# Top-32 attention: folding the scores twice before the search for the 32nd largest

## The chip, the cores and the metric

One core of a Trainium2 chip. The metric is the device time of one execution in microseconds, as the median of the runs shown.

## What is computed

Eight batches of eight heads, 576 tokens, head dimension 64. In every row of scores all but the 32 largest are masked, the rest goes through softmax and meets V. A feed-forward with a squared ReLU follows. Cut to what matters:

```python
scores = scale * np.matmul(q, k.transpose(0, 1, 3, 2))
kth = np.partition(scores, -32, axis=-1)[..., -32:-31]
scores = np.where(scores >= kth, scores, -1000000000.0)
attn = softmax(scores) @ v                  # (8, 8, 576, 64)
x = attn.transpose(0, 2, 1, 3).reshape(4608, 512)
out = np.maximum(x @ w_in, 0.0) ** 2 @ w_out    # 512 -> 2048 -> 512
```

So for each of 8 x 8 x 576 rows the 32nd largest of 576 numbers is needed, exactly.

## The kernel before

The kernel is written as a plan. `build` (L363) records every operation with its engine, an assumed duration, a priority (a due time), the tiles it reads, writes and takes, and the operations it must follow. `Plan.schedule` (L117) plays the plan through once, on the host, with the assumed durations, and thereby lays down the order of instructions on each engine; each engine's list is then emitted in that order, with semaphore waits where an operation needs another engine's or its own earlier result (`Emitter`, L204). On the chip nothing is reordered any more: an engine that waits holds up all that stands behind it.

Work is cut into pairs of heads (32 of them, `load_pair`, L371) and row blocks of 128 query rows, nine a pair, 288 in all. A pair's blocks are handled in four groups (`top_k`, L424): three with two blocks, the last with three (the third holds the 64 remaining rows of both heads). For a group:

- TensorE (PE) computes the scores into PSUM, ScalarE (ACT) copies them to `s` (L456), 128 x 576 in fp32.
- VectorE (DVE) takes `m`, the maximum of the left and the right half of `s` (L479), 288 columns. GpSimd (POOL) gets the minima as exact integers on the bit patterns: the sum of the halves `t1` (L476), and `lo` = `t1` - `m` (L482).
- On `m` DVE runs four rounds of MAX8 (L489, the eight largest of each row, sorted) with three MATCH_REPLACE8 between them (L494, these eight overwritten by -3e38): 32 largest of the maxima, in `a`. Each MATCH_REPLACE8 comes with a short MATCH_VALUE_LOAD. One MAX8 on `lo` (L500) gives the eight largest minima, `b8all`.
- A tiny minimum and a tiny reduction (L508, L511) merge the two sorted lists into `kth`, the 32nd largest of all 576, for the whole group.
- ACT makes the mask `w` from `s` and `kth` (L519).

`attend` (L538) adds the mask on PE in the transposed scores, ACT takes exp, PE multiplies with V; ACT copies the result (`av`), DVE takes a reciprocal of the row sums (`rzall`, L622), POOL multiplies (`x`, L624), PE transposes. `feed` (L644) is the feed-forward of a batch, spread over the next batch's top-k work; its squares run on ACT, in the last two batches on POOL (L678), at the very end on DVE. POOL also casts V (`vb`, L417, L420) and, in the first batch, the weights (L770).

`verdict` (L774) raises a flag if any row's result could be wrong (the eighth minimum is over the 32nd found); then a second, full program of the same tiling is run, which makes no such assumption. `PER` (L354) is the time per block by which priorities are spaced.

Of the kernel before, what the change touches and what calls it, by code (L numbers as in the profile page):

```python
# [12 lines left out]
P = 128  # L13
# [71 lines left out]
class Plan:  # L85
# [3 lines left out]
    def op(self, eng, dur, prio, fn, r=(), w=(), u=(), take=(), after=(), order=(), sem=None, ndma=0, nbf=0.0):  # L89
# [13 lines left out]
        for t in list(r) + list(w) + list(u):  # L103
            t.ops.append(o)
            t.left += 1
# [4 lines left out]
        o.later = ({t.taker for t in list(r) + list(w) + list(u)} | set(order)) - deps - {o, None}  # L110
        o.deps = deps
        o.wars = [t for t in list(w) + list(u)]
        o.tiles = list(r) + list(w) + list(u)
# [163 lines left out]
def bass_top_k_attn__then__act_relu_squared_kernel(  # L277
# [10 lines left out]
    HALF = S // 2  # L288
# [9 lines left out]
    def sb(name, shape, dt=FP32, n=None):  # L298
# [8 lines left out]
    b8all = sb("b8all", [P, NALL, 8])  # L307
    kth = sb("kth", [P, NALL])
# [45 lines left out]
    PER = 3.65  # L354
# [8 lines left out]
    def build(full, weights, pl):  # L363
        state = {"n": 0, "u": 0}
# [59 lines left out]
        def top_k(gi, qk, tg, dw):  # L424
# [36 lines left out]
            bt = tile("b") if full else None  # L461
            m, wk, t1, lo = ([tile(nm) for _ in range(nb)] for nm in ("m", "wk", "t1", "lo"))
            dk = [0]

            def dve(dur, fn, **kw):
                dk[0] += 1
                return pl.op("dve", dur, tg + .37 * dk[0], fn, **kw)

            def A(i, r):
                return at(a)[:, i, 8 * r:8 * r + 8]  # L470

            def B(i, r):
# [12 lines left out]
            last = [None] * nb  # L485
            for rnd in range(4):
                src = m if rnd == 0 else wk
                for i in range(nb):
                    last[i] = dve(.365, lambda i=i, rnd=rnd, src=src: vec.max(A(i, rnd), at(src[i])[:, :]),  # L489
                                  r=[src[i]], w=[a])  # L490
                if rnd == 3:
                    break
                for i in range(nb):
                    f = lambda i=i, rnd=rnd, src=src: vec.match_replace(  # L494
                        at(wk[i])[:, :], A(i, rnd), at(src[i])[:, :], NEG)
                    if rnd == 0:
                        dve(.425, f, r=[m[i]], w=[wk[i]], take=[wk[i]], after=[last[i]])
                    else:
                        dve(.425, f, u=[wk[i]], after=[last[i]])
            bl = [dve(.365, lambda i=i: vec.max(B(i, 0), at(lo[i])[:, :]), r=[lo[i]], w=[bt] if full else [])  # L500
                  for i in range(nb)]
            if full:
                bl = [dve(.425, lambda i=i: vec.match_replace(at(lo[i])[:, :], B(i, 0), at(lo[i])[:, :], NEG),
                          u=[lo[i]], after=[bl[i]]) for i in range(nb)]
                bl = [dve(.365, lambda i=i: vec.max(B(i, 1), at(lo[i])[:, :]), r=[lo[i]], w=[bt], after=[bl[i]])
                      for i in range(nb)]
            nr = 16 if full else 8
            mn = dve(.1, lambda: vec.tensor_tensor(  # L508
                at(a)[:, 0:nb, 32:32 + nr], at(bt)[:, 0:nb, 0:16] if full else b8all[:, n0:n0 + nb, :],
                at(a)[:, 0:nb, 30:30 - nr:-1], ALU.min), u=[a], r=[bt] if full else [], after=bl)  # L510
            kt = dve(.1, lambda: vec.tensor_reduce(  # L511
                kth[:, n0:n0 + nb], at(a)[:, 0:nb, 31:32 + nr], AX.X, ALU.max, negate=full), r=[a], after=[mn])
            kths.append(kt)
# [357 lines left out]
```

## Time and profile before

| | |
|---|---|
| median of 3 runs | 1114.63 us (1114.40 to 1114.79) |
| the profiled execution, its own time | 1116.01 us |
| its span (first to last instruction) | 1114.2 us |
| DVE busy | 1054.0 us (95%) |
| PE busy | 936.5 us (84%) |
| ACT busy | 772.7 us (69%) |
| POOL busy | 614.4 us (55%) |
| mean granted TensorE clock | 0.945 of full speed |

Busy times are unions of an engine's instructions; an instruction that has been issued and is held up inside its engine counts as busy. The profile's line of an operation is the line of the kernel before; a lambda's line is the line of the instruction in it.

### The profile page before, as it was taken

Reading aid. Unit: us, or ns where it says so; the run is one execution under the profiler, and the core shown is the slowest. Engines: PE = TensorE matmul, PEld = TensorE weight load, DVE = VectorE, ACT = ScalarE, POOL = GpSimd, SP = SyncE. Lnnn points to the kernel's source line nnn. Section 1 sums busy time; section 2 is a strip of 40 time slices with the busy share of each in tenths; the row PEclk is TensorE's granted clock in tenths of the full one; section 3 lists DMA queues with packets and bytes.
Section 4 is the critical chain, followed back from the end, with each engine's and each line's share of the span. In section 5 each row is a group of like instructions: output and inputs, shape, how many; then the busy total and the mean of one; then the engine's idle time right before and its main releaser. Section 6 shows DMA issues by size and latency. Waiting matters only on the chain.

```text
span 1114.2 us, 23090 instructions
## 1 busy us (share of the span) xinstructions
PE 936.5 (84%) x8082; PEld 551.0 (49%) x8082; DVE 1054.0 (95%) x3791; ACT 772.7 (69%) x1341; POOL 614.4 (55%) x815
## 2 busy tenths in 40 slices
PE   5767667989888997979878998888978899679997
PEld 3444434545455454645545554554445455445554
DVE  5999999999999999999999999999999999999961
ACT  4555657866788667976778676796678866567562
POOL 6775554555645555455545555545555455676461
PEclk8788888999989999999989999999998999989999
DMA  6851110111301121010301022011111000000001
GB/s 165 229 165 33 34 26 7 33 31 35 76 3 31 41 69 33 12 32 30 90 12 33 29 54 59 2 34 51 52 39 33 2 29 16 1 1 11 30 16 37
DMA packets 124414, 47.73 MB, mean 43 GB/s; under 512 B 116608, under 2 KB 116608, under 8 KB 124288
## 3 DMA queue, kind: packets, MB, share of 16 engines
q1 hardware_dynamic: 124288, 46.16, 16.2%
q8 instruction: 65, 1.06, 0.4%
q14 instruction: 61, 0.50, 0.2%
HBM read 36.70 MB, written 9.44 MB: 41 GB/s over the span
## 4 chain that ended last, share of the span: by engine, by line
DVE 79%; PE 14%; ACT 4%; issue 1%; DMA 1%; POOL 1%; SPq 0%; POOLq 0%
DVE a L489 31%; DVE wk L494 27%; PE ps L358 13%; DVE m L479 10%; DVE b8all L500 8%; ACT w L519 2%; DVE a L508 1%; DVE kth L511 1%; ACT s L456 1%; DVE rzall L622 1%; DMA rq<-in_q_dram 1%; POOL lo L482 0%; ACT av L620 0%; SPq L377 0%; DMA rk<-in_k_dram 0%
## 5 line engine op out<-in xcount | busy, mean ns | idle before, releaser
L358 PE MATMUL ps<-qk 64*128 64x288 f32 (+7 forms) x2640 | 442.9, 448 | 81.7 <-ACT s L456 42.2
L482 POOL TENSOR_TENSOR lo<-t,m 128x288 int32<-128x288 int32 x288 | 251.1, 887 | 330.9 <-DVE a L508 240.0
L489 DVE MAX8 a<-wk 128x8 f32<-128x288 f32 x864 | 344.9, 442 | 0.0
L358 PEld LDWEIGHTS ps<-qk 64*128 64x128 f32 (+1 forms) x2640 | 219.6, 187 | 204.6 <-ACT s L456 59.8
L519 ACT ACTIVATE w<-s,kth 128x576 bf16<-128x576 f32 x288 | 214.4, 771 | 123.4 <-DVE kth L511 122.9
L494 DVE MATCH_REPLACE8 wk<-a,wk 128x288 f32<-128x288 f32 x576 | 249.1, 438 | 0.0
L476 POOL TENSOR_TENSOR t<-s 128x288 int32<-128x288 int32 x288 | 227.9, 807 | 22.3 <-ACT s L456 19.9
L581 ACT ACTIVATE p<-ps 128x640 bf16<-128x640 f32 (+1 forms) x192 | 154.7, 809 | 77.2 <-PE ps L358 76.5
L456 ACT COPY s<-ps 128x576 f32<-128x576 f32 x288 | 171.0, 641 | 37.5 <-PE ps L358 36.2
L358 PE MATMUL ps<-xt,win 128*128 128x288 bf16 (+2 forms) x1088 | 151.9, 290 | 25.3 <-ACT g L665 14.0
L479 DVE TENSOR_TENSOR m<-s 128x288 f32<-128x288 f32 x288 | 152.8, 531 | 13.4 <-ACT s L456 13.4
L358 PE MATMUL ps<-wo,g 128*128 128x512 bf16 (+1 forms) x640 | 161.9, 381 | 2.5 <-ACT s L456 2.2
L358 PEld LDWEIGHTS ps<-steep_bf,w 128*128 128x128 bf16 (+1 forms) x1600 | 83.6, 102 | 112.6 <-issue 111.7
L358 PEld LDWEIGHTS ps<-xt,win 128*128 128x128 bf16 x1088 | 97.4, 101 | 65.4 <-ACT g L665 17.4
L494 DVE MATCH_REPLACE8 wk<-a,m 128x288 f32<-128x288 f32 x288 | 124.6, 438 | 0.0
L358 PE MATMUL ps<-steep_bf,w 128*128 128x128 bf16 (+3 forms) x1600 | 124.1, 222 | 0.0
L489 DVE MAX8 a<-m 128x8 f32<-128x288 f32 x288 | 115.8, 442 | 0.2
L500 DVE MAX8 b8all<-lo 128x8 f32<-128x288 f32 x288 | 114.8, 439 | 0.0
L624 POOL TENSOR_TENSOR x<-av,rzall 128x256 bf16<-128x256 f32 (+2 forms) x68 | 44.9, 660 | 78.5 <-DVE rzall L622 72.9
L358 PEld LDWEIGHTS ps<-wo,g 128*128 128x128 bf16 (+1 forms) x640 | 54.3, 100 | 60.2 <-issue 11.8
L665 ACT ACTIVATE g<-ps 128x576 bf16<-128x576 f32 x112 | 72.5, 649 | 13.6 <-PE ps L358 12.8
L358 PE MATMUL ps<-vb,p 128*128 128x65 bf16 (+1 forms) x1600 | 62.8, 195 | 6.1 <-ACT p L594 6.0
(52 smaller groups left out, 641.1 us busy)
## 6 DMA issues: line engine op xcount, KB each, us to landing
rq<-in_q_dram SPq DMA_DIRECT2D x64, 128.0 KB, 2.4
rk<-in_k_dram SPq DMA_DIRECT2D x64, 128.0 KB, 2.5
rv<-in_v_dram SPq DMA_DIRECT2D x64, 128.0 KB, 2.4
out_dram<-o SPq DMA_DIRECT2D x32, 256.0 KB, 2.0
ws<-in_moe_w_in_dram SPq DMA_DIRECT2D x8, 512.0 KB, 4.4
ws<-in_moe_w_out_dram SPq DMA_DIRECT2D x8, 512.0 KB, 4.4
rq<-in_q_dram SPq DMA_DIRECT2D x32, 32.0 KB, 2.4
rk<-in_k_dram SPq DMA_DIRECT2D x32, 32.0 KB, 2.5
```

The source lines that it names most:

```text
L358: return pe.matmul(o, l, r, start=start, stop=stop, skip_group_check=True)
L456: pl.op("act", .64, tg - 28 + i, lambda i=i: act.copy(at(st[i])[:, :].rearrange("p (a c) -> p a c", a=2), ps32[:, ss[i].slot:ss[i].slot + ...
L476: pl.op("gp", .81, tg - 1 + .8 * i, lambda i=i: gp.tensor_tensor(at(t1[i])[:, :].bitcast(I32), at(st[i])[:, 0:HALF].bitcast(I32), at(st[i] ...
L479: dve(.42, lambda i=i: vec.tensor_tensor(at(m[i])[:, :], at(st[i])[:, 0:HALF], at(st[i])[:, HALF:S], ALU.max), r=[st[i]], w=[m[i]], take=[ ...
L482: pl.op("gp", .88, tg + .8 + .8 * i, lambda i=i: gp.tensor_tensor(at(lo[i])[:, :].bitcast(I32), at(t1[i])[:, :].bitcast(I32), at(m[i])[:, ...
L489: last[i] = dve(.365, lambda i=i, rnd=rnd, src=src: vec.max(A(i, rnd), at(src[i])[:, :]), r=[src[i]], w=[a])
L494: f = lambda i=i, rnd=rnd, src=src: vec.match_replace(at(wk[i])[:, :], A(i, rnd), at(src[i])[:, :], NEG)
L500: bl = [dve(.365, lambda i=i: vec.max(B(i, 0), at(lo[i])[:, :]), r=[lo[i]], w=[bt] if full else []) for i in range(nb)]
L519: pl.op("act", .75, tw + .8 * i, lambda i=i: act.activation(at(ws[i])[:, :], at(st[i])[:, :], ACTF.Relu, bias=kth[:, n0 + i:n0 + i + 1], s ...
L581: return act.activation(o, i, ACTF.Exp, scale=0.125)
L624: pl.op("gp", .15 + .16 * nu, tt + 4, lambda: gp.tensor_tensor(at(xr)[:, 0:nu, :], at(avs)[:, 0:nu, 0:64], rzall[:, u0:u0 + nu].unsqueeze( ...
L665: return act.activation(at(g)[:, 0:nt].rearrange("p (a c) -> p a c", a=2), ps32[:, hh.slot:hh.slot + 2, 0:hw], ACTF.Relu)
```

## The change

Scores are folded twice. DVE takes `m` as before and then `pp`, the maximum of the two halves of `m` (144 columns: the largest of each four scores). POOL builds both kinds of minima by integer sum and subtraction: `t2` = sum of the halves of `m`, the middle ones `t2` - `pp`, and the low ones `t1` - `m`. All three go into one tile `f` of 576 columns: what is left of `pp` in columns 0 to 143, the middle ones in 144 to 287, the low ones in 288 to 575.

The rounds: MAX8 and MATCH_REPLACE8 on `pp` (144 columns), again on `f[0:144]`, again on `f[0:288]` (after the middle minima are there), and a fourth MAX8 on all 576 (after the low ones), whose eighth is the 32nd largest. MAX8 writes its eight in reverse order into `kth`, so that the eighth stands in the block's column and the next block of its kind overwrites the other seven. L508 and L511 go. The flag is raised where `kth` is over the 16th or the 24th found. Each block's mask now waits for its own last MAX8. The pools of tiles change (`f` of 576 columns x 4, `pp` x 4, `m` 4 instead of 3, `t2` x 2; `wk`, `lo`, `b` go), `PER` is 3.2 instead of 3.65, and since durations and dependences changed the schedule lays all engines' orders down anew. The second program, which runs only when the flag is raised, gets four rounds on 576 columns. The core of the diff:

```diff
-        "s": ([P, S], FP32, 8), "m": ([P, HALF], FP32, 3), "wk": ([P, HALF], FP32, 3),
-        "t1": ([P, HALF], FP32, 2), "lo": ([P, HALF], FP32, 3), "a": ([P, 3, 48], FP32, 3),
-        "b": ([P, 3, 16], FP32, 2), "sh": ([P, 3], FP32, 2), "w": ([P, S], BF16, 13),
+        "s": ([P, S], FP32, 8), "m": ([P, HALF], FP32, 4), "pp": ([P, QUART], FP32, 4),
+        "t1": ([P, HALF], FP32, 2), "t2": ([P, QUART], FP32, 2), "f": ([P, S], FP32, 4),
+        "a": ([P, 3, 8], FP32, 3), "sh": ([P, 3], FP32, 2), "w": ([P, S], BF16, 13),
...
-    PER = 3.65
+    PER = 3.2
...
+            def eighth(t, i):
+
+                return t[:, i, ix[i] + 7:(ix[i] - 1 if ix[i] else None):-1]
...
-            for i in range(nb):
-                pl.op("gp", .81, tg - 1 + .8 * i, lambda i=i: gp.tensor_tensor(
-                    at(t1[i])[:, :].bitcast(I32), at(st[i])[:, 0:HALF].bitcast(I32),
-                    at(st[i])[:, HALF:S].bitcast(I32), ALU.add), r=[st[i]], w=[t1[i]], take=[t1[i]])
...
-                pl.op("gp", .88, tg + .8 + .8 * i, lambda i=i: gp.tensor_tensor(
-                    at(lo[i])[:, :].bitcast(I32), at(t1[i])[:, :].bitcast(I32),
-                    at(m[i])[:, :].bitcast(I32), ALU.subtract), r=[t1[i], m[i]], w=[lo[i]], take=[lo[i]])
-            for rnd in range(4):
...
+                def whole(dur, prio, i, op, o, x, y, **kw):
+                    return pl.op("gp", dur, prio + .8 * i, lambda: gp.tensor_tensor(
+                        o().bitcast(I32), x().bitcast(I32), y().bitcast(I32), op), **kw)
...
+                    whole(.81, tg - 1, i, ALU.add, L, A, B, r=[st[i]], w=[t1[i]], take=[t1[i]])
+                    dve(.42, lambda i=i, A=A, B=B: vec.tensor_tensor(at(m[i])[:, :], A(), B(), ALU.max),
+                        r=[st[i]], w=[m[i]], take=[m[i]])
...
+                    whole(.46, tg - .5, i, ALU.add, L, M1, M2, r=[m[i]], w=[t2[i]], take=[t2[i]])
+                    dve(.27, lambda i=i, M1=M1, M2=M2: vec.tensor_tensor(at(pp[i])[:, :], M1(), M2(), ALU.max),
+                        r=[m[i]], w=[pp[i]], take=[pp[i], f[i]] + ([a] if i == 0 else []))
+                for i in range(nb):
+                    mid.append(whole(.48, tg + .5, i, ALU.subtract, lambda i=i: at(f[i])[:, QUART:HALF],
+                                     lambda i=i: at(t2[i])[:, :], lambda i=i: at(pp[i])[:, :],
+                                     r=[t2[i], pp[i]], w=[f[i]]))
+                    low.append(whole(.88, tg + 2.5, i, ALU.subtract, lambda i=i: at(f[i])[:, HALF:S],
+                                     lambda i=i: at(t1[i])[:, :], lambda i=i: at(m[i])[:, :],
+                                     r=[t1[i], m[i]], w=[f[i]]))
...
+                    prev[i] = [dve(.215, lambda i=i: vec.max(at(a)[:, i, :], at(pp[i])[:, :]), r=[pp[i]], w=[a])]
...
+                    prev[i] = [dve(.275, lambda i=i: vec.match_replace(
+                        at(f[i])[:, 0:QUART], at(a)[:, i, :], at(pp[i])[:, :], NEG),
+                        r=[pp[i]], hold=[a], w=[f[i]], after=prev[i])]
+                for t, wd, dur, more in ((c16, QUART, .215, None), (c24, HALF, .365, mid)):
+                    for i in range(nb):
+                        prev[i] = [chain(t, i, prev[i] + ([more[i]] if more else []), dur,
+                                         lambda i=i, t=t, wd=wd: vec.max(eighth(t, i), at(f[i])[:, 0:wd]),
+                                         hold=[f[i]])]
+                    for i in range(nb):
+                        prev[i] = [chain(t, i, prev[i], dur + .06, lambda i=i, t=t, wd=wd: vec.match_replace(
+                            at(f[i])[:, 0:wd], eighth(t, i), at(f[i])[:, 0:wd], NEG), hold=[f[i]])]
+                for i in range(nb):
+                    ks.append(chain(kth, i, prev[i] + [low[i]], .665, lambda i=i: vec.max(
+                        eighth(kth, i), at(f[i])[:, :]), hold=[f[i]]))
```

What the schedule makes of it. A group of two blocks on DVE in the middle of the kernel before (`a` holds the eights, `wk` the worked-down maxima):

```order
L479 TENSOR_TENSOR m<-s 128x288
L508 TENSOR_TENSOR a<-b8all,a 128x2x8
L479 TENSOR_TENSOR m<-s 128x288
L511 TENSOR_REDUCE kth<-a 128x2
L489 MAX a<-m 128x8 x2
L494 MATCH_REPLACE wk<-a,m 128x288 x2
L489 MAX a<-wk 128x8 x2
L494 MATCH_REPLACE wk<-a,wk 128x288
L622 RECIPROCAL rzall<-av 128x5
```

L508 and L511 there belong to the group before. The same place after the change, a whole group (`c` stands for both c16 and c24, the eights of rounds two and three):

```order
L522 TENSOR_TENSOR m<-s 128x288 x2
L528 TENSOR_TENSOR pp<-m 128x144 x2
L539 MAX a<-pp 128x8 x2
L541 MATCH_REPLACE f<-a,pp 128x144 x2
L547 MAX c<-f 128x8 x2
L550 MATCH_REPLACE f<-c,f 128x144 x2
L547 MAX c<-f 128x8 x2
L550 MATCH_REPLACE f<-c,f 128x288 x2
L553 MAX kth<-f 128x8 x2
```

The four two-input instructions m, m, pp, pp now stand one behind the other at the head of a group; nothing is left of the merge at its end. POOL in the middle of the kernel before:

```order
L482 TENSOR_TENSOR lo<-t,m 128x288 x2
L476 TENSOR_TENSOR t<-s 128x288 x2
L417 CAST vb<-rv 128x8x64
L624 TENSOR_TENSOR x<-av,rzall 128x320
L420 TENSOR_SCALAR vb<-rv,heads 128x64 x2
```

And after (`t<-s` is the sum of the halves of s, `t<-m` that of the halves of m, `f<-t,pp` the middle and `f<-t,m` the low minima), from the low minima of a group of two through the head of the group of three behind it:

```order
L514 TENSOR_TENSOR f<-t,m 128x288
L663 TENSOR_TENSOR x<-av,rzall 128x320
L514 TENSOR_TENSOR f<-t,m 128x288
L514 TENSOR_TENSOR t<-s 128x288 x2
L419 CAST vb<-rv 128x8x64
L514 TENSOR_TENSOR t<-m 128x144 x2
L514 TENSOR_TENSOR f<-t,pp 128x144
L514 TENSOR_TENSOR t<-m 128x144
L514 TENSOR_TENSOR f<-t,pp 128x144 x2
```

Between a group's sums (done before its m) and its low minima, POOL now has the two instructions on 144 columns for each block. In the last batch the squares of the feed-forward (`g<-g`) stand among these, on POOL:

```order
L717 TENSOR_TENSOR g<-g 128x576
L514 TENSOR_TENSOR f<-t,m 128x288 x2
L663 TENSOR_TENSOR x<-av,rzall 128x320
L717 TENSOR_TENSOR g<-g 128x576 x3
L514 TENSOR_TENSOR t<-s 128x288
L514 TENSOR_TENSOR t<-m 128x144
L514 TENSOR_TENSOR t<-s 128x288
```

In the kernel before they stand in the same way between `lo` and `t1`, one or two at a time.

## Rows read from the trace of the kernel before

**Rows 1.** The page: busy us (share of the span) and instructions of each engine.
```profile
PE 936.5 (84%) x8082; PEld 551.0 (49%) x8082; DVE 1054.0 (95%) x3791; ACT 772.7 (69%) x1341; POOL 614.4 (55%) x815
```

**Rows 2.** Stretches of the span: length, busy us (x instructions) of PE, PEld, DVE, ACT, POOL; clock, DMA.
```profile
150.00:950.00 800.00, 699.32 (x6040) 407.36 (x6040) 793.92 (x2874) 596.57 (x1027) 424.83 (x558) 0.96 0.14 35
...
1000.00:1114.00 114.00, 103.83 (x996) 61.55 (x994) 77.20 (x272) 65.09 (x127) 54.06 (x71) 0.99 0.07 23
```

**Rows 3.** Timeline of DVE, 500 to 507 us: start, length, instruction.
```profile
501.05 0.07 DVE L494 MATCH_VALUE_LOAD wk<-a,wk 128x8 f32 x1
...
501.48 1.17 DVE L489 MAX8 a<-wk 128x8 f32<-128x288 f32 x3
502.56 0.07 DVE L494 MATCH_VALUE_LOAD wk<-a,wk 128x8 f32 x1
...
506.07 0.43 DVE L479 TENSOR_TENSOR m<-s 128x288 f32<-128x288 f32 x1
506.43 0.17 DVE L508 TENSOR_TENSOR a<-b8all,a 128x24 f32<-128x24 f32 x1
506.52 0.45 DVE L479 TENSOR_TENSOR m<-s 128x288 f32<-128x288 f32 x1
506.89 0.17 DVE L511 TENSOR_REDUCE kth<-a 128x3 f32<-128x27 f32 x1
```

**Rows 4.** Timeline of all engines, 495.4 to 497.5 us: DVE and POOL side by side.
```profile
495.41 0.45 DVE L479 TENSOR_TENSOR m<-s 128x288 f32<-128x288 f32 x1
495.49 1.03 POOL L482 TENSOR_TENSOR lo<-t,m 128x288 int32<-128x288 int32 x1 [3.77 <-DVE a L508]
...
495.86 0.97 DVE L479 TENSOR_TENSOR m<-s 128x288 f32<-128x288 f32 x1
...
496.59 0.89 POOL L476 TENSOR_TENSOR t<-s 128x288 int32<-128x288 int32 x1
...
496.75 1.17 DVE L489 MAX8 a<-m 128x8 f32<-128x288 f32 x3
497.44 1.55 POOL L482 TENSOR_TENSOR lo<-t,m 128x288 int32<-128x288 int32 x2
```

**Rows 5.** Groups of DVE: count | busy us, mean ns of one | idle us before them.
```profile
L479 DVE TENSOR_TENSOR m<-s 128x288 f32<-128x288 f32 x288 | 152.8, 531 | 13.4 <-ACT s L456 13.4
...
L511 DVE TENSOR_REDUCE kth<-a 128x3 f32<-128x27 f32 x32 | 5.5, 171 | 0.1
...
L779 DVE TENSOR_REDUCE fone<-fcmp 128x1 f32<-128x288 f32 x1 | 0.5, 453 | 0.0
```

**Rows 6.** Instructions on tile m: ns min/median/max, first and last start in us.
```profile
L479 DVE TENSOR_TENSOR m<-s x288: 427/446/1375, 11.4 to 1068.4; 128x288 f32<-128x288 f32 x144
```

**Rows 7.** Groups of POOL: columns as in rows 5.
```profile
L482 POOL TENSOR_TENSOR lo<-t,m 128x288 int32<-128x288 int32 x288 | 251.1, 887 | 330.9 <-DVE a L508 240.0 <-DVE m L479 82.4 <-DVE rzall L622 8.5
L476 POOL TENSOR_TENSOR t<-s 128x288 int32<-128x288 int32 x288 | 227.9, 807 | 22.3 <-ACT s L456 19.9
L420 POOL TENSOR_SCALAR vb<-rv,heads 128x64 bf16<-128x64 f32 x64 | 28.2, 452 | 0.0
L624 POOL TENSOR_TENSOR x<-av,rzall 128x320 bf16<-128x320 f32 x32 | 24.6, 768 | 10.2 <-DVE a L508 5.5 <-DVE rzall L622 4.7
L417 POOL CAST vb<-rv 128x512 bf16<-128x512 f32 x32 | 19.6, 612 | 35.0 <-PE ps L358 30.7 <-DMA rv<-in_v_dram 4.2
L678 POOL TENSOR_TENSOR g<-g 128x576 bf16<-128x576 bf16 x16 | 18.2, 1147 | 8.7 <-ACT g L665 8.5 <-DVE wk L494 0.2
L624 POOL TENSOR_TENSOR x<-av,rzall 128x256 bf16<-128x256 f32 x28 | 17.1, 612 | 47.3 <-DVE rzall L622 47.3
L678 POOL TENSOR_TENSOR g<-g 128x320 bf16<-128x320 bf16 x16 | 12.0, 761 | 0.7 <-ACT g L667 0.7
...
L770 POOL CAST win<-ws 128x1024 bf16<-128x1024 f32 x8 | 8.1, 1037 | 2.2 <-DMA ws<-in_moe_w_in_dram 2.2
...
L624 POOL TENSOR_TENSOR x<-av,rzall 128x128 bf16<-128x128 f32 x8 | 3.2, 394 | 20.9 <-DVE rzall L622 20.9
```

More of the change, by code (lines that the diff above doesn't have):

```diff
@@ L87, in __init__, with op @@
         self.ops = []
-    def op(self, eng, dur, prio, fn, r=(), w=(), u=(), take=(), after=(), order=(), sem=None, ndma=0, nbf=0.0):
+    def op(self, eng, dur, prio, fn, r=(), w=(), u=(), hold=(), take=(), after=(), order=(), sem=None, ndma=0, nbf=0.0):
         o = Op()
@@ L102, in op @@
             deps.update(t.ops)
-        for t in list(r) + list(w) + list(u):
+        for t in list(r) + list(w) + list(u) + list(hold):
             t.ops.append(o)
@@ L109, in op @@
             t.taker = o
-        o.later = ({t.taker for t in list(r) + list(w) + list(u)} | set(order)) - deps - {o, None}
+        o.later = ({t.taker for t in list(r) + list(w) + list(u) + list(hold)} | set(order)) - deps - {o, None}
         o.deps = deps
-        o.wars = [t for t in list(w) + list(u)]
-        o.tiles = list(r) + list(w) + list(u)
+        o.wars = list(w) + list(u)
+        o.tiles = list(r) + list(w) + list(u) + list(hold)
         self.ops.append(o)
@@ L306, in bass_top_k_attn__then__act_relu_squared_kernel @@
     steep_bf = sb("steep_bf", [P, P], BF16)
-    b8all = sb("b8all", [P, NALL, 8])
-    kth = sb("kth", [P, NALL])
+    kth = sb("kth", [P, 3, 4 * NPAIR + 8])
+    c16 = sb("c16", [P, 3, 4 * NPAIR + 8])
+    c24 = sb("c24", [P, 3, 4 * NPAIR + 8])
     rzall = sb("rzall", [P, NALL])
@@ L363, in build @@
     def build(full, weights, pl):
-        state = {"n": 0, "u": 0}
+        state = {"n": 0, "u": 0, "g": 0, "z": 0, "last": {}}
         kths, rzs = [], []
@@ L460, in top_k @@
             a = tile("a")
-            bt = tile("b") if full else None
-            m, wk, t1, lo = ([tile(nm) for _ in range(nb)] for nm in ("m", "wk", "t1", "lo"))
             dk = [0]
+            ix = [state["g"], state["g"], state["z"]]
+            state["g"] += 1
+            state["z"] += nb == 3
             def dve(dur, fn, **kw):
                 dk[0] += 1
-                return pl.op("dve", dur, tg + .37 * dk[0], fn, **kw)
-            def A(i, r):
-                return at(a)[:, i, 8 * r:8 * r + 8]
@@ L485, in top_k @@
-            last = [None] * nb
-            for rnd in range(4):
-                src = m if rnd == 0 else wk
-                for i in range(nb):
[L489 to L492, printed above, removed]
-                for i in range(nb):
[L494 to L513, printed above, removed]
+                return pl.op("dve", dur, tg + .34 * dk[0], fn, **kw)
@@ L514, in top_k @@
+            kths.extend(ks)
             tw = tg + PER * nb + dw
@@ L776, in verdict @@
         t = Tile(psum)
-        c = pl.op("dve", .35, 1e6, lambda: vec.tensor_tensor(
-            fcmp[:, :], b8all[:, :, 7], kth[:, :], ALU.is_gt), after=kths)
-        d = pl.op("dve", .35, 1e6, lambda: vec.tensor_reduce(fone[:, 0:1], fcmp[:, :], AX.X, ALU.max), after=[c])
+        G = 4 * NPAIR
+        done = kths
+        for ls, lo_, hi in ((slice(0, 2), 0, 2 * G), (slice(2, 3), 2 * G, 2 * G + NPAIR)):
+            fc = fcmp[:, lo_:hi].rearrange("p (l g) -> p l g", l=ls.stop - ls.start)
+            g = (hi - lo_) // (ls.stop - ls.start)
+            x = pl.op("dve", .3, 1e6, lambda ls=ls, g=g, fc=fc: vec.tensor_tensor(
+                fc, c16[:, ls, 0:g], c24[:, ls, 0:g], ALU.min), after=kths)
+            done = done + [pl.op("dve", .3, 1e6, lambda ls=ls, g=g, fc=fc: vec.tensor_tensor(
+                fc, kth[:, ls, 0:g], fc, ALU.is_gt), after=[x])]
+        d = pl.op("dve", .35, 1e6, lambda: vec.tensor_reduce(fone[:, 0:1], fcmp[:, :], AX.X, ALU.max), after=done)
         e = pl.op("dve", .35, 1e6, lambda: vec.tensor_reduce(fone[:, 1:2], rzall[:, :], AX.X, ALU.max), after=rzs)
```

60 lines of the change are left out of this document (47 added, 13 removed).

## Prediction

> **What bounds the kernel now.** I read the page first. VectorE (DVE) is busy 1054.0 of 1114.2 us (95%), PE 84%, ScalarE 69%, GpSimd (POOL) 55% [rows 1]. From 150 to 950 us DVE is busy 793.92 of 800 us [rows 2], so the middle of the kernel is a queue of DVE work, and the time falls if that queue gets shorter. PE has 699.32 busy in the same 800 us, POOL 424.83.
>
> Next, what an instruction costs in that queue. A recorded duration is longer than the step to the next instruction: three MAX8 of 288 columns, begun at 501.48, are over after 1.17, but the next instruction starts at 502.56. So each holds the queue for 0.36 and is 0.45 long. A value load with its MATCH_REPLACE8 takes 0.43, a free maximum m 0.36, the small merge L508 0.09 [rows 3], and I give its reduction L511 the same. Per row block (128 rows of scores; 288 of them) that is 0.36 + 5 x 0.36 + 3 x 0.43 + 0.18 x 128/288 = 3.53 us.
>
> The last view is the one that matters for this change: DVE and POOL side by side [rows 4]. The second m starts 0.37 us into a POOL subtraction. The POOL instruction ends at 496.52, and the next DVE instruction starts at 496.75: this m held its queue for 0.89 instead of 0.36 (and so got in 0.13 before the other's recorded end). The other way round, that subtraction started 0.08 into the first m and lasted 1.03, while the two undisturbed ones at the end of these rows take 1.55, 0.78 each: it began its work 0.32 after that m's start. So a two-input DVE instruction and a two-input POOL instruction exclude each other, and who comes second waits until the first is done. MAX8 shows none of it: the three at 496.75, beside POOL's work, take the 1.17 of the three in [rows 3]. Today this costs little: m has a mean of 531 and a median of 446 ns [rows 5, 6], 85 ns x 288 = 24 us, because POOL mostly sits idle until DVE is past its maxima: its subtractions sit behind waits of 240.0 us for L508 and 82.4 for m [rows 7].
>
> **DVE's own work.** How cost goes with columns: a TENSOR_REDUCE takes 171 ns at 27 columns and 453 at 288 [rows 5], 1.08 ns a column. So 144 columns fewer save 0.156 us and 288 more cost 0.31. Per block:
> - m stays, 0.36; the second fold pp is new, 144 columns: 0.36 - 0.156 = 0.205. No row has this shape; it can't be under 0.09 (the tiny L508) nor over 0.36.
> - five MAX8 become four: 0.205 + 0.205 + 0.36 + (0.36 + 0.31) = 1.44 instead of 1.80.
> - three replacements: 2 x (0.43 - 0.156) + 0.43 = 0.98 instead of 1.29.
> - the minimum and the reduction of L508/L511 go: -0.08. The threshold is now written by the last MAX8 itself, whose reversed eight outputs I cost at nothing.
>
> That is 2.985 instead of 3.53, and 0.545 x 288 = **-157 us**.
>
> The Trainium skill ("VectorE: DVE Perf Modes", The DRAIN you can't avoid) says that the next operation does not start until the pipe is empty. The rows differ: 0.45 long, 0.36 apart [rows 3]. Costed by that page, every instruction saved would give 0.08 more, about 20 us over the kernel as an estimate; I don't count it.
>
> **POOL's new work.** A block now needs four two-input POOL instructions instead of two: the sum of halves (0.75 behind another, 807 ns long) and its subtraction, and the same on 144 columns. For 144 columns the nearest rows are the multiply x at 394 ns (128 columns) and 612 (256) [rows 7], 1.7 ns a column: about 0.42, up to half of 0.887, which is 0.44. I take 0.45 long, 0.41 back to back; the outer bound is the 0.8 of a 288-column one. POOL gets 2 x 0.41 x 288 = 236 us more: 850 in all.
>
> **The two together.** This is where I expect half of the gain to go. The order shows m, m, pp, pp on DVE against t2, t2, mid, mid, low, low, sum, sum on POOL (t2 adds the halves of m, mid and low are the subtractions). With the two rules of [rows 4], from the start of the first m: the second m runs until 0.72; t2 of the first block asks at 0.43, gets in at 0.67, ends at 1.12 and lets the next one in 0.12 before that; pp waits for it and is past at 1.21; the second t2 is already asking and goes first, to 1.61; the second pp is past at 1.70. Free, the four would be past at 1.13: 0.57 lost. In a group of three, the same alternation puts the last pp at 2.54 instead of 1.70: 0.84 lost. A pair of heads has three groups of two and one of three, nine blocks: 3 x 0.57 + 0.84 = 2.55, or 0.283 a block. The 0.085 of today goes, so 0.2 x 288 = **+57 us**.
>
> After pp, POOL of a two-block group needs until 5.6 us (mid 2.5, low 4.0, both sums of the next group 5.6); DVE's seven remaining rounds end at 1.70 + 4.84 = 6.54. The waits for mid (needed at 3.64) and low (needed at 5.22) therefore cost nothing. A pair takes DVE 3 x 6.54 + 9.9 = 29.5 and POOL 3 x 5.6 + 9.4 plus what else it has (a cast 0.61, one of two scalings 0.45 and one x 0.77) 28.0. POOL is at 95%: whenever it is behind, a sum still runs when the next m starts. For half of the 128 groups I add half a sum, 0.35: **+22 us**.
>
> **Where POOL has other work.** In the first batch 16 weight casts of 1.04 us [rows 7] add 16.6 us; POOL's spare in four pairs is 6, so **+10**. In the last batch the squares of the feed-forward stand in POOL's order between the subtractions that DVE waits for: 16 of 1.147 and 13 of 0.761 us, 28 us, with some 5 us spare, partly at the end, where DVE idles today too (77.20 busy of 114 [rows 2]): **+20**.
>
> Sum: 1114.2 - 157 + 57 + 22 + 10 + 20 = 1066 us of span. This execution took 1116.0 in all, the median of the runs is 1114.63, about its span; I take **1066 us**.
>
> PE, ACT and the DMAs keep their instructions. PE's 936.5 us in 1066 is 88%, and the 800 us of [rows 2] would be some 740 (2.985 + 0.283 + 0.076 = 3.34 a block instead of 3.53 + 0.085) with 699 of PE in them, 94%. That is why I expect no more than this, and a shorter time would meet PE next.
>
> **Rivals.**
> - *The exclusion hardly bites.* If pp usually slips in before POOL asks, DVE needs 27 us a pair, and today's 24 us go too: 1114 - 157 - 24 + 30 = 963. But PE's 699 in the 800 us would then have to fit into 660, so it goes at PE's pace, 40 us more: about 1005. For it: today most m are free. Against it: today POOL waits for DVE; after the change it seldom would. Chance 0.14.
> - *Three engines near full in a fixed order.* POOL 95% and PE 94% with orders laid down in advance: x on POOL waits for DVE's reciprocal, 4.7 + 47.3 + 20.9 = 72.9 us today [rows 7], which idle POOL time hides and which now would push the subtractions late. If another 0.12 us a block is lost this way, 35 us, the time is 1100. Chance 0.2.
> - *Slower: POOL becomes the bound.* The place is POOL's eight instructions a group. If a 144-column POOL instruction costs nearly what a 288-column one does, because starting it dominates, POOL's pair grows by 18 x 0.36 = 6.5 to 34.5 us, 3.83 a block, against 3.67 in today's kernel (1057 us from the first m to the last [rows 6], for 288 blocks). That is 1114 + 288 x 0.16 + 30 = 1190. It decides from about 0.7 us for the 144-column form. For it: POOL is the one engine whose new shape I have no row of. Against: x falls from 768 to 612 to 394 ns with its columns [rows 7]. With milder forms of it, chance 0.11.
> - *The flag.* The kernel has a second program for rows that its folding gets wrong. It is run if the 24 scores taken before the last round are not all among the 32 largest; for that about nine of a row's 32 largest would have to be minima of their pairs. Of 32 picks among 288 pairs (496 couples of picks, each a pair with a chance of 1 in 575) about one is. Then the time would double; chance under 0.01.
>
> The Trainium skill ("Advanced Engine Details and Errata", VectorE Performance Modes) says that the second Vector port is shared with GpSimd, so that GpSimd and 2-port Vector instructions block each other, and lists no 2-port mode for tensor_tensor. By that section alone m and pp would be free, which is the first rival and about 1005 us. By that rule the trace disagrees, 0.89 instead of 0.36 [rows 4]; another line of the page, under GPSIMD Details, does name instructions with two SBUF inputs.
>
> **How the numbers follow.** The forecast's case (1045 to 1085) has 0.55, the rivals 0.14, 0.2, 0.11. The range from **1010 to 1112** takes in the first two rivals and leaves out the slower one and the tails. What a measurement of this kernel can tell from no change is about 0.2%. Faster by more than that: 0.55 + 0.14 + 0.17 = **0.86**; within: **0.03**; slower: **0.11**.
>
> **What would show it.** In the profile after: MAX8 of 144, 288 and 576 columns about 0.29, 0.44 and 0.75 us long; the int32 forms of 144 columns near 0.45; m and pp with means well over their medians; DVE still busy over 93% (it counts waiting for POOL as busy), POOL near 80%. I am wrong if pp and m are as short as when free, if POOL's 144-column form is over 0.6, if DVE sits idle in front of MAX8 for POOL, or if PE's idle time is gone.

## The result, and the profile after

| | before | after |
|---|---|---|
| median of the runs | 1114.71 us | 1081.69 us (1080.86 to 1085.84, 4 runs) |
| ratio | | 0.9703, 95% interval 0.967 to 0.9737 |
| span of the profiled execution | 1114.2 us | 1079.0 us |
| DVE busy | 1054.0 us | 980.8 us |
| PE busy | 936.5 us | 918.1 us |
| POOL busy | 614.4 us | 906.7 us |

Faster by 3.0%, 33 us; forecast were 48. The time lies between the forecast (1066) and the second rival (1100). The page after (busy us, share of the span, instructions; and the chain that ended last, by engine and by line), against [rows 1]:

```profile
PE 918.1 (85%) x8035; PEld 548.5 (51%) x8082; DVE 980.8 (91%) x3538; ACT 765.9 (71%) x1341; POOL 906.7 (84%) x1391
...
DVE 59%; POOL 13%; PE 12%; issue 10%; ACT 5%; SPq 0%; DMA 0%; POOLq 0%; DVEq 0%
DVE kth L553 15%; PE ps L360 12%; DVE c L547 11%; DVE m L522 10%; DVE f L550 8%; POOL f L514 7%; DVE pp L528 7%; POOL t L514 5%; DVE f L541 4%; DVE a L539 3%; ACT w L561 2%; ACT s L458 1%; POOL x L663 1%; PE ps L363 1%; DVE rzall L661 1%
```

The chain of before, by engine:

```profile
DVE 79%; PE 14%; ACT 4%; issue 1%; DMA 1%; POOL 1%; SPq 0%; POOLq 0%
```

POOL went from 55 to 84%, DVE from 95 to 91%, and POOL, which had 1% of the chain that ended last, now has 13% of it. DVE's groups after (count | busy us, mean ns | idle us before them), against [rows 5]:

```profile
L553 DVE MAX8 kth<-f 128x8 f32<-128x576 f32 x288 | 202.9, 742 | 2.6 <-POOL f L514 2.6
L522 DVE TENSOR_TENSOR m<-s 128x288 f32<-128x288 f32 x288 | 158.8, 583 | 40.8 <-ACT s L458 40.8
L528 DVE TENSOR_TENSOR pp<-m 128x144 f32<-128x144 f32 x288 | 131.5, 492 | 0.4
...
L547 DVE MAX8 c<-f 128x8 f32<-128x288 f32 x288 | 117.8, 443 | 1.9 <-POOL f L514 1.9
...
L541 DVE MATCH_REPLACE8 f<-a,pp 128x144 f32<-128x144 f32 x288 | 81.4, 287 | 0.0
L539 DVE MAX8 a<-pp 128x8 f32<-128x144 f32 x288 | 73.8, 292 | 0.1
```

The new widths cost what the columns said: MAX8 is 292 ns long at 144 columns and 742 at 576. But the two maxima m and pp are far over their free length. pp has 144 columns like the MAX8 of 292 ns, and lasts 492; m lasts 583 where it was 531 [rows 5]. POOL's four kinds of two-input instructions, against [rows 7]:

```profile
L514 POOL TENSOR_TENSOR t<-s 128x288 int32<-128x288 int32 x288 | 234.0, 823 | 33.0 <-ACT s L458 30.5
L514 POOL TENSOR_TENSOR f<-t,m 128x288 int32<-128x288 int32 x288 | 228.1, 807 | 0.0
L514 POOL TENSOR_TENSOR t<-m 128x144 int32<-128x144 int32 x288 | 180.8, 638 | 49.9 <-DVE m L522 47.8
L514 POOL TENSOR_TENSOR f<-t,pp 128x144 int32<-128x144 int32 x288 | 141.7, 509 | 3.2 <-DVE pp L528 3.2
```

The same exclusion from the other side: the sum t2 of 144 columns (`t<-m`) lasts 638 ns, the subtraction on as many columns 509. And the head of a group of two, in the timeline (start, length, instruction), as the prediction replayed it:

```profile
370.88 0.80 DVE L522 TENSOR_TENSOR m<-s 128x288 f32<-128x288 f32 x2
371.40 1.15 POOL L514 TENSOR_TENSOR t<-m 128x144 int32<-128x144 int32 x2 [0.40 <-DVE m L522]
371.61 1.11 DVE L528 TENSOR_TENSOR pp<-m 128x144 f32<-128x144 f32 x2
...
372.51 0.55 POOL L514 TENSOR_TENSOR f<-t,pp 128x144 int32<-128x144 int32 x1
372.64 0.51 DVE L539 MAX8 a<-pp 128x8 f32<-128x144 f32 x2
```

Free, the two m and two pp take 1.13 us. Here the first MAX8 starts 1.76 us after the first m, which is also the median of the trace's groups of two without idle time; 1.70 was worked out. The two pp stand for 1.11 us, half of it waiting for POOL's `t<-m`.

From the start times of the trace I made an account of DVE between its first m and its last MAX8: own work (each kind's count times its step to the next instruction when free), waits inside m, pp and their like (mean step less the free 0.358 us at 288 and 0.209 at 144 columns), and idle time. Left out are the 11 us before the first m and some 5 us of steps a little over the free ones.

| us | before | after | difference | forecast |
|---|---|---|---|---|
| own work | 1017 | 869 | -148 | -157 |
| waits of two-input instructions for POOL | 29 | 103 | +74 | +57 + 22 |
| idle | 14 | 60 | +46 | +10 + 20, for POOL's other work |
| after the last MAX8 | 39 | 31 | -8 | |

Idle time came in lumps, most where DVE wants scores or row sums that ACT has not delivered: of the 60 us, 30 stand in front of m and 24 in front of the reciprocal; before the change it was 2 and 11. Three stretches of the trace after (length, then busy us of PE, PEld, DVE, ACT, POOL, each with its count; clock, DMA share, GB/s), and the waits of the whole span (us in total, times, longest; the 40.8 at m include 11.1 before the first m):

```profile
150.00:200.00 50.00, 41.01 (x397) 26.31 (x395) 48.33 (x170) 38.39 (x66) 40.68 (x66) 0.98 0.11 25
200.00:250.00 50.00, 42.14 (x348) 24.08 (x350) 35.39 (x125) 35.59 (x64) 38.08 (x61) 0.99 0.27 65
250.00:300.00 50.00, 43.92 (x398) 26.38 (x398) 50.00 (x188) 35.06 (x62) 44.81 (x69) 0.97 0.18 44
```

```profile
PE ps L363 <- POOL x L663: 55.7, 37, 7.3
...
POOL x L663 <- DVE rzall L661: 43.9, 32, 7.5
DVE m L522 <- ACT s L458: 40.8, 10, 13.4
...
DVE rzall L661 <- ACT av L659: 28.9, 12, 7.9
...
DVE kth L553 <- POOL f L514: 2.6, 1, 2.6
```

At 218 us m waits 13.4 us for `s`; DVE is busy 35.39 of those 50 us. PE stands 55.7 us in front of x, POOL 43.9 us in front of DVE's reciprocal, DVE 28.9 us in front of the row sums that PE and ACT make. The waits that I had costed at nothing, MAX8 for POOL's minima, are next to nothing: 2.6 us, and 1.9 at the middle ones.

### The profile page after: what moved, and what is told of

Same layout as the page of the kernel before. It is cut to its first block, busy times and chain, and to the rows that moved or that the text cites. A ratio compares the mean times of both kernels' runs of the same rounds, so it can differ in the third digit from the quotient of the medians.

```text
span 1079.0 us, 23727 instructions
## 1 busy us (share of the span) xinstructions
PE 918.1 (85%) x8035; PEld 548.5 (51%) x8082; DVE 980.8 (91%) x3538; ACT 765.9 (71%) x1341; POOL 906.7 (84%) x1391
## 4 chain that ended last, share of the span: by engine, by line
DVE 59%; POOL 13%; PE 12%; issue 10%; ACT 5%; SPq 0%; DMA 0%; POOLq 0%; DVEq 0%
DVE kth L553 15%; PE ps L360 12%; DVE c L547 11%; DVE m L522 10%; DVE f L550 8%; POOL f L514 7%; DVE pp L528 7%; POOL t L514 5%; DVE f L541 4%; DVE a L539 3%; ACT w L561 2%; ACT s L458 1%; POOL x L663 1%; PE ps L363 1%; DVE rzall L661 1%
## 5 line engine op out<-in xcount | busy, mean ns | idle before, releaser
L514 POOL TENSOR_TENSOR f<-t,m 128x288 int32<-128x288 int32 x288 | 228.1, 807 | 0.0
L514 POOL TENSOR_TENSOR t<-m 128x144 int32<-128x144 int32 x288 | 180.8, 638 | 49.9 <-DVE m L522 47.8
L550 DVE MATCH_REPLACE8 f<-c,f 128x144 f32<-128x144 f32 (+1 forms) x576 | 206.4, 363 | 0.0
L553 DVE MAX8 kth<-f 128x8 f32<-128x576 f32 x288 | 202.9, 742 | 2.6 <-POOL f L514 2.6
L522 DVE TENSOR_TENSOR m<-s 128x288 f32<-128x288 f32 x288 | 158.8, 583 | 40.8 <-ACT s L458 40.8
L547 DVE MAX8 c<-f 128x8 f32<-128x144 f32 (+1 forms) x576 | 190.8, 367 | 2.0 <-POOL f L514 1.9
L360 PE MATMUL ps<-wo,g 128*128 128x512 bf16 (+1 forms) x593 | 151.5, 383 | 8.7 <-ACT p L620 2.1
L360 PE MATMUL ps<-xt,win 128*128 128x288 bf16 (+2 forms) x1088 | 142.9, 284 | 7.4 <-ACT g L706 2.4
L514 POOL TENSOR_TENSOR f<-t,pp 128x144 int32<-128x144 int32 x288 | 141.7, 509 | 3.2 <-DVE pp L528 3.2
L528 DVE TENSOR_TENSOR pp<-m 128x144 f32<-128x144 f32 x288 | 131.5, 492 | 0.4
L541 DVE MATCH_REPLACE8 f<-a,pp 128x144 f32<-128x144 f32 x288 | 81.4, 287 | 0.0
L663 POOL TENSOR_TENSOR x<-av,rzall 128x256 bf16<-128x256 f32 (+2 forms) x68 | 43.7, 643 | 44.6 <-DVE rzall L661 43.9
```

The costliest lines, as they stand in the source:

```text
L360: return pe.matmul(o, l, r, start=start, stop=stop, skip_group_check=True)
L514: return pl.op("gp", dur, prio + .8 * i, lambda: gp.tensor_tensor(o().bitcast(I32), x().bitcast(I32), y().bitcast(I32), op), **kw)
L522: dve(.42, lambda i=i, A=A, B=B: vec.tensor_tensor(at(m[i])[:, :], A(), B(), ALU.max), r=[st[i]], w=[m[i]], take=[m[i]])
L528: dve(.27, lambda i=i, M1=M1, M2=M2: vec.tensor_tensor(at(pp[i])[:, :], M1(), M2(), ALU.max), r=[m[i]], w=[pp[i]], take=[pp[i], f[i]] + ([ ...
L541: prev[i] = [dve(.275, lambda i=i: vec.match_replace(at(f[i])[:, 0:QUART], at(a)[:, i, :], at(pp[i])[:, :], NEG), r=[pp[i]], hold=[a], w=[ ...
L547: lambda i=i, t=t, wd=wd: vec.max(eighth(t, i), at(f[i])[:, 0:wd]),
```

## The experiments

**Is it POOL's work on 144 columns?** Its two instructions left out:

```diff
-                    whole(.46, tg - .5, i, ALU.add, L, M1, M2, r=[m[i]], w=[t2[i]], take=[t2[i]])
...
-                    mid.append(whole(.48, tg + .5, i, ALU.subtract, lambda i=i: at(f[i])[:, QUART:HALF],
...
+        fzero = [] if full else [pl.op("dve", .3, -94, lambda t=t: vec.memset(t[:, QUART:HALF], NEG)) for t in mem["f"]]
```

> Left out: POOL's sum and subtraction on 144 columns; the middle minima are never computed and stand at -3e38, so the rows' thresholds are too low. DVE's instructions on the scores are those of the changed kernel. Exclusion theory (m and pp wait for POOL's two-input instructions): pp falls from a step of 0.416 us to about 0.22, m from 0.517 to about 0.42, and with POOL no longer full DVE's idle time between its first and last block falls from 60 to under 25 us; 970 to 1010 us in all, where PE becomes the next limit. Rival (narrow instructions and the order of the rounds are dear in themselves): pp stays over 0.35 and the time over 1050.

1043.66 us, in the one execution there is. The waits of m and pp fell from 103 to 62 us, not to the 20 or so that I expected, and idle time from 60 to 52, not to under 25. Neither case came: the time is over the 970 to 1010 of the first and under the 1050 of the rival. pp is still far from its free 0.29 us:

```profile
L528 DVE TENSOR_TENSOR pp<-m 128x144 f32<-128x144 f32 x288 | 111.6, 426 | 0.3
```

POOL's low subtraction had moved up into the place of the instructions left out: it can start as soon as m is there, which is just when pp runs. By the start times, 28 of pp's 41 us of waits stand beside it. So the new instructions account for 41 of the 103 us, and the rest stays without them. The next two runs separate how much POOL does from where it stands.

**What stands beside the two-input instructions?** In both runs DVE makes the middle minima itself, and POOL keeps two instructions a block, as before the change. In the second run one dependence is added.

```diff
+                    mid.append(dve(.27, lambda i=i, M1=M1, M2=M2: vec.tensor_tensor(
+                        at(f[i])[:, QUART:HALF], M1(), M2(), ALU.min), r=[m[i]], w=[f[i]]))
```

> The middle minima come from one DVE minimum of 144 columns instead of POOL's sum and subtraction. DVE gets 288 x 0.21 = 60 us of own work, POOL loses some 300 us busy. Exclusion theory: three two-input instructions a block now meet only POOL's sum of halves and low subtraction; together they lose about 0.15 to 0.25 us a block instead of 0.36, and DVE's idle time falls by 30 us: 1045 to 1070 us. Rival (only DVE's own work counts, POOL's load does not): 1081 + 60 = 1140 us.

And, in the second run alone:

```diff
-                                     r=[t1[i], m[i]], w=[f[i]]))
+                                     r=[t1[i], m[i]], w=[f[i]], after=[mid[-1]]))
```

> As the run with the middle minima on DVE, and the low subtraction of a group waits for the group's last two-input DVE instruction, so that POOL's two-input work falls into the rounds. Exclusion theory: the two-input instructions run free (m 0.36, pp and the minimum 0.21), no more than 0.08 us a block is lost, 1000 to 1035 us. Rival (the waits come from POOL being busy at all, whatever its order): same time as the run without the added dependence, within 0.5%.

Measured: **1276.16 us** (ratio 1.1427, 1.1408 to 1.1446) without the dependence, **1043.51 us** (0.934, 0.9324 to 0.9356) with it. My expectation for the first was wrong by 200 us, and its rival (1140) by 136. The second lies 8.5 us over its range (1000 to 1035), with 0.12 us a block of waits where 0.08 was the most expected; its rival, the time of the run without the dependence, is out. POOL was busy 49% and 57% of the two spans, DVE's own work was the same 930 us, and the waits were 275 us in the one and 36 in the other. The head of a group without the dependence:

```profile
508.80 0.79 POOL L514 TENSOR_TENSOR f<-t,m 128x288 int32<-128x288 int32 x1 [1.91 <-DVE m L522]
509.31 0.60 DVE L522 TENSOR_TENSOR m<-s 128x288 f32<-128x288 f32 x1
509.83 1.11 DVE L527 TENSOR_TENSOR pp<-m 128x144 f32<-128x144 f32 x2
509.98 0.79 POOL L514 TENSOR_TENSOR f<-t,m 128x288 int32<-128x288 int32 x1 [0.39 <-DVE m L522]
...
510.74 1.68 POOL L514 TENSOR_TENSOR t<-s 128x288 int32<-128x288 int32 x2
510.87 1.71 DVE L529 TENSOR_TENSOR f<-m 128x144 f32<-128x144 f32 x2
```

Here POOL's `f<-t,m` and `t<-s` stand opposite m, pp and the minimum one for one; two minima of 144 columns take 1.71 us, two pp 1.11. With the dependence, the same two minima and POOL's next instructions:

```profile
499.93 0.52 DVE L529 TENSOR_TENSOR f<-m 128x144 f32<-128x144 f32 x2
...
500.36 0.51 DVE L537 MAX8 a<-pp 128x8 f32<-128x144 f32 x2
500.52 1.56 POOL L514 TENSOR_TENSOR f<-t,m 128x288 int32<-128x288 int32 x2 [3.41 <-DVE f L529]
...
502.03 0.81 POOL L514 TENSOR_TENSOR t<-s 128x288 int32<-128x288 int32 x1
```

0.52 for two, and POOL's subtractions fall into the MAX8 rounds. DVE's groups without and with it, in that order:

```profile
L529 DVE TENSOR_TENSOR f<-m 128x144 f32<-128x144 f32 x288 | 200.8, 729 | 0.0
L527 DVE TENSOR_TENSOR pp<-m 128x144 f32<-128x144 f32 x288 | 171.1, 626 | 0.2
L522 DVE TENSOR_TENSOR m<-s 128x288 f32<-128x288 f32 x288 | 170.9, 602 | 33.9 <-ACT s L458 33.9
```

```profile
L522 DVE TENSOR_TENSOR m<-s 128x288 f32<-128x288 f32 x288 | 140.7, 497 | 31.2 <-ACT s L458 31.2
...
L527 DVE TENSOR_TENSOR pp<-m 128x144 f32<-128x144 f32 x288 | 84.4, 325 | 0.2
...
L529 DVE TENSOR_TENSOR f<-m 128x144 f32<-128x144 f32 x288 | 79.0, 306 | 0.0
```

So what costs is not how busy POOL is, but whether its two-input instructions stand opposite DVE's. A dependence that makes POOL wait (3.41 us in front of the two subtractions above) takes 230 us off the kernel.

**The same idea with POOL's eight instructions kept.** The sum of m's halves and the low subtraction wait for the group's last pp:

```diff
+                    whole(.46, tg - .5, i, ALU.add, lambda i=i: at(t2[i])[:, :], M1, M2, r=[m[i]], w=[t2[i]],
+                          take=[t2[i]], after=[pps[-1]])
...
+                                     r=[t1[i], m[i]], w=[f[i]], after=[pps[-1]]))
```

> The changed kernel with one dependence added: the sum of the halves of m and the low subtraction of a group wait for the group's last pp. DVE's two-input instructions then stand together and POOL's follow. Exclusion theory in its simple form (it is the alternation at the head of a group that costs): pp falls to 0.22, the time to about 1045. Rival (POOL is nearly full, and any time it waits at the head of a group comes back as late sums, late x and waits of DVE for the minima): 1075 to 1110 us, with more waits of MAX8 for POOL.

1077.94 us (0.9652, 0.9618 to 0.9685), the rival. The waits at pp halved, from 59 to 30 us, those at m grew from 44 to 59, idle time from 60 to 67, and in it that of MAX8 for POOL from 4.5 to 11 us. With four instructions a block POOL has no room: what it doesn't do at a group's head it does at the next one's m.

**Each half of the change alone.** One fold as before, with the new rounds and without the merge; `pp`, `t2` and the middle minima are gone:

```diff
-                for t, wd, dur, more in ((c16, QUART, .215, None), (c24, HALF, .365, mid)):
+                for t, wd, dur, more in ((c16, HALF, .365, None), (c24, HALF, .365, None)):
```

> The other half of the change alone: one fold as before, three rounds on 288 columns in a tile of 576, the fourth MAX8 on all 576 after the low minima, no merge. DVE's own work is 0.358 + 3 x (0.36 + 0.427) + 0.667 + 0.02 = 3.41 us a block, 34 us less than before; POOL as before. If m meets POOL no more often than before (28 us of waits), about 1080 us, that is, as fast as with both folds. If the fold's own work counts alone, 1114 - 34 = 1080 too, but then the second fold should have given 110 us more and did not.

**1058.86 us** (0.9461, 0.9433 to 0.9489): faster than the whole change, and 21 us under the 1080 expected. DVE's own work is 977 us, 40 less than before where 34 were expected, and m hardly loses anything to POOL any more:

```profile
L522 DVE TENSOR_TENSOR m<-s 128x288 f32<-128x288 f32 x288 | 120.0, 459 | 22.6 <-ACT s L458 22.6
```

```profile
POOL f L514 <- DVE m L522: 329.8, 118, 4.5
```

And the m of a group of three, with POOL's first low subtraction:

```profile
503.01 1.18 DVE L522 TENSOR_TENSOR m<-s 128x288 f32<-128x288 f32 x3
503.53 1.31 POOL L514 TENSOR_TENSOR f<-t,m 128x288 int32<-128x288 int32 x1 [1.85 <-DVE m L522]
```

459 ns is 20 over its free length: 6 us of waits instead of 29. POOL's subtraction waits for m about as long as it did before (240.0 + 82.4 [rows 7]), so that alone is not the reason. The start times show where the difference lies: before, 19 us of the waits were at the 38 m that stand right behind the reduction L511, as the m at 495.86 in [rows 4] does. Here the merge is gone, 152 of the 288 m follow another m directly, and these lose 3 us together; the one that waits is POOL, as in the last line, 1.31 us long where two undisturbed ones take 1.55 [rows 4].

Set against this, the second fold takes 108 us of DVE's own work away (977 to 869) and brings 97 us of waits (6 to 103) and 35 us of idle time (25 to 60). It is a loss of 21 us of span (27 us by the two ratios).

**The plan's durations.** The plan took pp for 0.27 and t2 for 0.46 us; here it is told the measured steps.

```diff
-    PER = 3.2
+    PER = 3.45
...
-                    dve(.27, lambda i=i, M1=M1, M2=M2: vec.tensor_tensor(at(pp[i])[:, :], M1(), M2(), ALU.max),
+                    dve(.42, lambda i=i, M1=M1, M2=M2: vec.tensor_tensor(at(pp[i])[:, :], M1(), M2(), ALU.max),
```

> The changed kernel; only the plan's assumed durations are replaced by the steps measured in its trace (m 0.52, pp 0.42, sum of m's halves 0.60, low 0.78, priorities every 3.45 us a block). If the fixed order is bad because the plan believed the two-input instructions to be free (the rival of three full engines in a fixed order), DVE's idle time falls from 60 to under 35 us and the time to about 1055. If the exclusion itself is what costs, whatever the order, the waits of m and pp stay near 100 us and the time within 1% of 1081.

1050.68 us (0.9397, 0.9381 to 0.9412). Idle time fell from 60 to 39 and the time to about the 1055 of the first case, though not under its 35 us of idle time; of the second case the waits held (97), and the time did not. The instructions are the same, so some 31 us of the change's time (34 by the two ratios) were in the order.

**The weight casts.**

```diff
-            weights.append(pl.op("gp", 1.1, 40 + 6 * i, lambda s=s, dst=dst, view=view: gp.tensor_copy(dst, view(s)),
+            weights.append(pl.op("act", 1.0, 40 + 6 * i, lambda s=s, dst=dst, view=view: act.copy(dst, view(s)),
```

> The changed kernel with the 16 weight casts of the first batch on ScalarE instead of GpSimd. If POOL's load in the first batch delays the feed-forward and with it the scores (DVE's idle 13.4 us at 218 us), that gap goes and the time falls by 15 to 25 us. If not, within 0.5% of the changed kernel.

1069.16 us (0.9561, 0.9539 to 0.9583): 1.4% less by the two ratios, about the size expected, but for another reason. The gap of 13.4 us shrank to 3.4, others of 8 to 11 us came up later, and idle time as a whole stayed (66). The waits fell from 103 to 86, 7 of these 17 us in the first batch.

**The ring of row sums.** The reciprocal, x, the transposes and their copy due 6 us later:

```diff
-            rz = pl.op("dve", .1, tt + 4, lambda: vec.reciprocal(rzall[:, u0:u0 + nu], at(avs)[:, 0:nu, 64]), r=[avs])
+            rz = pl.op("dve", .1, tt + 10, lambda: vec.reciprocal(rzall[:, u0:u0 + nu], at(avs)[:, 0:nu, 64]), r=[avs])
```

> The changed kernel with the chain of the row sums (reciprocal on DVE, x on POOL, the transposes on PE, their copy) due 6 us later in the plan, so that DVE and PE reach them when their inputs have long been there. If DVE's 46 us more of idle time come from engines that stand in front of an instruction of this ring too early (DVE before the reciprocal, PE before x and so late with the scores), its idle time falls from 60 to under 35 us and the time to about 1055; the waits of m and pp stay near 100 us. If the idle time only moves to other places when the orders are laid down anew, it stays between 45 and 75 us and the time within 1% of 1081.

1088.61 us (0.9747, 0.9721 to 0.9772). The rival: DVE's waits for the row sums fell from 28.9 to 18.8 us, those for scores rose from 40.8 to 52.5, those of the middle MAX8 for POOL from 1.9 to 10.6, and idle time is 67.

**Towards a faster version.** From the run with the dependence (1043.51 us), the sum of the halves of s also after the two-input instructions:

```diff
+                    whole(.81, tg + 1, i, ALU.add, lambda i=i: at(t1[i])[:, :], A, B, r=[st[i]], w=[t1[i]],
+                          take=[t1[i]], after=[mid[-1]])
```

> As the run with the middle minima on DVE and the low subtraction after the group's two-input DVE instructions, and now also the sum of the halves of s waits for them. Exclusion theory: what is left of the waits (18.6 us at m, 11.5 at pp, 5.9 at the minimum) falls below 15 together, 1010 to 1030 us, where PE (some 920 us busy) becomes the next limit. Rival: POOL's work comes too late for the last MAX8, which then waits for the low minima; 1045 us or more.

**1028.39 us** (0.9188, 0.9172 to 0.9203), with 30 us of waits left, where under 15 were expected, and 27 idle; 13 of the 30 fall in the last batch, where POOL has the squares. It beats both kernels. Then the plan's durations set to the free ones (m 0.38, pp and the minimum 0.22, POOL's two 0.77, a block every 3.3), which puts the groups one behind the other:

> As the run with both POOL instructions of a block after the group's two-input DVE instructions, with the plan's durations set to the free steps of the trace (m 0.38, pp and the minimum 0.22, sum and subtraction 0.77, priorities every 3.3 us a block). In the order no m of the next group stands between the last rounds of this one any more, as some did. Exclusion theory: the 30 us of waits at m, pp and the minimum fall below 12; 1000 to 1018 us. If what is left there comes from x and the squares on POOL, or PE is the limit already, within 0.7% of 1028.

1062.01 us (0.9509, 0.9477 to 0.9541). A miss: the waits stayed at 30 us, and idle time doubled, from 27 to 54. DVE now stands in front of the row sums, 46.3 us in total (12.8 at most) where the run before it stood 14.1:

```profile
DVE rzall L661 <- ACT av L659: 46.3, 13, 12.8
```

The last two: the casts on ACT on top of that order, and the late reciprocal on top of the 1028 us version.

> As the run with the clean order, with the 16 weight casts of the first batch on ScalarE. With POOL at some 58% its casts should no longer matter: within 0.5% of that run. If the casts hold up the feed-forward or the masks, 8 to 15 us less.

1054.09 us (0.9437, 0.9406 to 0.9468): 0.8% less, the lower end of its second case; the waits fell from 30 to 25, idle time not at all.

> The fastest version so far (middle minima on DVE, sum and low subtraction after the two-input DVE instructions, 1028 us) with the same chain due 6 us later. If the ring is what idles DVE, its 27 us there fall below 18 and the time to 1010 to 1020. If not, within 1% of 1028 or above.

1028.55 us (0.9215, 0.9197 to 0.9233): no change. Idle time 22 instead of 27, the waits 33 instead of 30.

## Why the prediction was right, and where not

- *DVE's own work, -157 us*: -148. By columns it came out as worked out; the steps of the narrow forms are 0.21 (MAX8), 0.28 (replacement with its load) and 0.67 us (576 columns).
- *POOL's 144-column form, 0.45 us*: 0.49 where nothing stands against it (median of the middle subtractions). A little low. The mean of the sums, 0.64, is over the 0.6 that was a sign of being wrong, but by waiting and not by its own cost, which is far from the 0.7 from which the slower rival decides.
- *The exclusion, +57 and +22*: +74. The mechanism and the size hold. A head of two measured 1.76 us against 1.70. The runs with and without the added dependence show that it is this: the same instructions, 275 against 36 us of waits. The rule was drawn too narrowly in two places: POOL's one-input casts hold up m and pp as well (below), and the two don't always alternate as in the replay. In the run without the 144-column work only 66 of the 288 pp were held by over 0.06 us; among the others are many beside POOL's low subtraction, and there it was POOL that waited. What decides which goes first the runs don't show. Of the signs, DVE at 91% missed its 93%, and pp's mean (492 ns) lies under its median (589), since more than half of the pp were held.
- *Waits for the middle and low minima at nothing*: 4.5 us.
- *POOL's other work, +10 and +20*: this is the step that failed, in size. I put all further loss into casts and squares, in the first and the last batch. The casts are worth some 16 us (the run with casts on ACT, by the ratios), though by fewer waits and not by less idle time. The last batch lost 19 us to waits at m and pp where the middle ones lose 10, and 12 us of idle time, 8 more than before. But most of the +46 idle lies in the batches between, where I had nothing: 16 us in the second, 13 in the fourth, 6 and 7 in the sixth and seventh. There DVE, POOL and PE each stand in front of an instruction whose input another of them owes. That was the second rival, at 35 us, and the kernel took part of it. The 13.4 us lump of the second batch went down to 3.4 when the casts moved, so part of it may belong to the casts; that is not shown.
- *POOL at 95%*: the working counts one scaling and one x a pair of heads, where [rows 7] have 64 scalings and 68 x for the 32 pairs. That is another 1.1 us a pair: POOL at 29.1 of DVE's 29.5 us, and a spare of 1.6 us in four pairs instead of 6. By these rows POOL was about as full as DVE, which speaks for the second rival.
- *After the last MAX8* the kernel needs 8 us less than before. The prediction had no term for it; that this made up for part of the idle time is luck.
- *The first rival* (the exclusion hardly bites, 1005 us) fell: 103 us of waits. *The flag* did not come up.
- PE as the next limit: no run came so far. At 1028 us PE is busy 917 us, 89%.

What stays open: why DVE idles 60 us in one order of these instructions and 39 in another. Telling the plan the measured durations took 21 us off here, and the same kind of correction put 27 on in another version; the late reciprocal moved the idle time from the row sums to the scores and to POOL's middle minima, and its sum did not fall. Each of these lays all five orders down anew, and no run kept the orders and changed one place. So it is shown that the idle time changes with the order alone, and not which instruction of the ring begins a stall.

I also had the direction of the design half wrong without saying so: I took the second fold for the source of the gain. Alone, the new rounds without merge gave 1058.86 us, and the second fold gave 21 us of it back.

## What to carry to other kernels

Two engines that exclude each other are to be planned as one resource: before moving work to the idle one, see what it will stand opposite to, and place it beside instructions that don't exclude it. A dependence that makes the helper wait can be worth more than a lighter helper (230 us here). And where a change has two parts, time each alone: here the simple half beat the whole.

## What the runs showed of the hardware

A DVE instruction with two SBUF inputs can lose far more than it costs, to an engine that is half idle: in the run of 1276 us, with POOL busy 49%, the minimum of 144 columns took a mean of 729 ns instead of some 290, pp 626. The Trainium skill ("GPSIMD Engine Reference", Key points) names contention of GpSimd with Vector instructions of two SBUF inputs. The trace agrees, and shows its size: in the 1276 us run a pp and a minimum hold DVE for 0.81 and 0.82 us in the median instead of 0.21, about as long as the POOL instruction opposite (0.79). The Trainium skill's rule that I weighed ahead of the result, which knows only 2-port modes ("Advanced Engine Details and Errata", VectorE Performance Modes), would have made m and pp free; in the trace after, 130 of the 288 m and 165 of the 288 pp hold DVE for over 0.06 us more than when free.

POOL's instruction needs no second input for this. In the first batch of the 1043 us run two pp, 0.52 us when free, stand beside two weight casts:

```profile
58.23 2.39 POOL L807 CAST win<-ws 128x1024 bf16<-128x1024 f32 x2
58.59 2.19 DVE L527 TENSOR_TENSOR pp<-m 128x144 f32<-128x144 f32 x2
```

MAX8 on 144 columns was not touched: 292 ns after the change with POOL busy 84%, and 292 in the 1276 us run with POOL at 49%.

On the gap between DVE instructions the prediction set the rows against the Trainium skill ("VectorE: DVE Perf Modes", The DRAIN you can't avoid). The same section adds that a next operation which is not held starts earlier, so rows 0.45 long and 0.36 apart [rows 3] need not go against it.
